# A decode step of four interleaved layers: the second attention layer's first queries split by key head, and a wider down product in the first feed-forward block

## The chip, the cores and the metric

The kernel runs on one core of one Trainium2 chip. The metric is the device time of one execution in microseconds; lower is better.

## The reference

Four layers run one after another on a residual `x` of 4 batch elements, one position each, 512 wide: attention, feed-forward, attention, feed-forward. Both attention layers use the same weights and the same key and value cache, and so do both feed-forward layers.

```python
def _A_ref(x, k_cache, v_cache, wq, wo):      # x [4, 1, 512]
    q = (x @ wq).reshape(B, Sq, 32, 128).transpose(0, 2, 1, 3)
    k = jnp.repeat(k_cache, 4, axis=1)        # caches [4, 8, 4096, 128]
    v = jnp.repeat(v_cache, 4, axis=1)
    scores = jnp.einsum("bhqd,bhkd->bhqk", q, k) * (128 ** -0.5)
    p = _softmax(scores, axis=-1)
    o = jnp.einsum("bhqk,bhkd->bhqd", p, v)
    return o.transpose(0, 2, 1, 3).reshape(B, Sq, 4096) @ wo

def _B_ref(x, w_gate, w_up, w_down):          # 512 -> 1792 -> 512
    return (_gelu(x @ w_gate) * (x @ w_up)) @ w_down

x = x + _A_ref(_layernorm(x), ...)
x = x + _B_ref(_layernorm(x), ...)
x = x + _A_ref(_layernorm(x), ...)
x = x + _B_ref(_layernorm(x), ...)
```

All inputs are bf16. Each batch element has 8 key heads of 4096 positions; four query heads share a key head.

## The kernel before, in words

**Order of the work.** An element depends on no other, so the kernel goes element by element: attention of element 0 (`attend_first`), its feed-forward block (`dense_first`), then `attend`, which does layer 3 of element 0 and layer 1 of element 1 together, then element 1's feed-forward block, and so on. Keys of an element stay in SBUF between its two attention layers; most values are read twice. The order of all instructions on each engine is the order in which they are written; the program doesn't reorder them.

**Tiles.** The 8 key heads of an element are two groups of four (`GH`). A head's 4096 positions are two tiles, `t = 0` and `t = last = 1`, of 128 x 2048 bf16 (512 KB). A key tile, once loaded, is transposed in place by VectorE (`Keys.turn`, L537). `place` says in which buffer (`kw`, `kp`) a tile lives; `own` in `Early` keeps the places of element 0, whose tiles are still to be used when element 1's tiles have been given a place. `Keys.load` issues a load on SP's queue (L518), the V ring does so at L708. Loads of one queue are issued in order. Eight semaphores go round, so at most eight loads are outstanding.

**Scores.** `scores_of` (L592) multiplies tiles by masked queries in `qb`: four matmuls (`be`) for each head and tile, of 512 columns each, and head `s` of a group writes partitions 32s to 32s+31 of the bank `sc`. For a run of several heads the loop goes over `be` outside and heads inside. The masked queries come in three steps: `q_round` (L335) subtracts the mean's part and rounds on VectorE, `q_sums_of` (L353) makes 16 small matmuls with the identity, and `q_spread` (L360) multiplies by a mask on VectorE. `soft` is the softmax: L602 reduces `sc`, and L614 takes the exponentials.

**Around the change.** `dense_first` ends with `down`: 14 blocks of four matmuls (L275) that add `wd_sb` times `H_bf` into a PSUM tile `y2`. `wide` repeats the right side to 32 equal columns, of which one is used. `wd_sb` is loaded in five pieces that end after blocks 6, 10, 12, 13 and 14 (`WD_PARTS`). Then element 0's second layer begins. `Early` serves this one place: before `queries`, three key tiles of element 1 have been loaded into buffers that had been parked elsewhere, and no further load can be issued until scores of element 0 have read a tile. `queries` makes the queries of the first group: heads 2 and 3 of the group with 32 matmuls, then heads 0 and 1 with 32. `scores` lets the scores of tile 0 of heads 2 and 3 go first, loads two tiles of element 1 into their places, finishes the masked queries of heads 0 and 1 (`rest`), makes the second group's queries (`qy`, L309), scores the other tiles and issues three more loads; it also brings parked tiles back with copies on VectorE, GpSimd and ScalarE (L565, L568, L570).

`Norm` holds the layer norm of one element: its constructor copies the mean, `root` (two VectorE and two ScalarE instructions) makes the inverse root, `scales` the two factors that the softmax uses.

`acc` takes a PSUM bank of two that go round; `y2`, the queries' sums, `sc` of the first group and the second group's query rows all come from it.

Of the kernel before, what the change touches and what calls it, by code (L numbers as in the profile page):

```python
# [15 lines left out]
P = 128  # L16
# [4 lines left out]
WIDE = 32  # L21
WEIGHT = 64
# [3 lines left out]
GH = 4  # L26
# [4 lines left out]
WD_PARTS = (0, 6, 10, 12, 13, 14)  # L31
# [5 lines left out]
def kernel(  # L37
# [15 lines left out]
    _, Hkv, Sk, Dh = A_k_cache.shape  # L53
    HqDh = A_wq.shape[1]
    Hq = HqDh // Dh
    rep = Hq // Hkv
    F = B_w_gate.shape[1]
    assert B == RUN and Sq == 1 and Dh == P and rep == QD and Hkv % GH == 0
    KD = D // P
# [31 lines left out]
    wq_sb = [wts.tile([P, KD, HG * Dh], BF16, name=f"wq_sb{g}") for g in range(NG)]  # L91
# [3 lines left out]
    wd_sb = wts.tile([P, KF, D], BF16, name="wd_sb")  # L95
# [28 lines left out]
    def k_tile(i, t):  # L124
        pair, n = place[i, t]
        return pair[:, n]

    def acc(shape, name, t=None):
        if t is None:
            t = ps_ac.tile([P, 512], FP32, name=name, tag="acc")  # L130
        n = 1
        for s in shape:
            n *= s
        if len(shape) == 1:
            return t[:, :n]
        return t[:, :n].rearrange("p (a b) -> p a b", b=shape[1])

    def wide(v, width=WIDE):
        n = v.shape[-1]
        return v.unsqueeze(1).broadcast_to([P, width // n, n])  # L140
# [133 lines left out]
    def mac(dst, lhsT, rhs, first, last):  # L274
        nc.tensor.matmul(dst, lhsT=lhsT, rhs=rhs, start=first, stop=last, skip_group_check=True)  # L275
# [54 lines left out]
    def q_tile():  # L330
        return grp.tile([P, HG], BF16, name="q_bf", tag="q_bf", bufs=1)

    def q_round(q_bf, q, g, norm, h0=0):
        own = slice(h0, h0 + q.shape[1])
        nc.vector.scalar_tensor_tensor(out=q_bf[:, own], in0=cs_q[:, g, own], scalar=norm.mean,  # L335
                                       in1=q[:, :, 0], op0=ALU.mult, op1=ALU.subtract)
# [4 lines left out]
    def q_sum_tile():  # L341
        return ps_sm.tile([P, GH, BE, rep], FP32, name="qe", tag="sm")

    def q_sums(q):
        qe = q_sum_tile()
        q_sums_of(qe, q, 0, GH)
        return qe

    def q_sums_of(qe, q, s0, n):
        iv = ident_bf[:].rearrange("p (b w e) -> p b e w", b=NB, e=2)  # L350
        for be in range(BE):
            for a in range(QD):
                nc.tensor.matmul(qe[a * QS:(a + 1) * QS, s0:s0 + n, be], lhsT=iv[:, be // 2, be % 2],  # L353
                                 rhs=q[:, s0 * rep:(s0 + n) * rep], start=True, stop=True,
                                 skip_group_check=True)

    def q_spread(qe, s0=0, n=GH):
        dst = qb[:, W:].rearrange("p (n x a h) -> p n x a h", x=2, a=QD, h=rep)[:, :, 0]
        shape = [P, n * BE, QD, rep]
        nc.vector.tensor_tensor(  # L360
            out=dst[:, s0 * BE:(s0 + n) * BE],
            in0=qe[:, s0:s0 + n].rearrange("p s n h -> p (s n) h").unsqueeze(2).broadcast_to(shape),
            in1=amask.unsqueeze(1).unsqueeze(3).broadcast_to(shape),
            op=ALU.mult)
# [11 lines left out]
    class OutProj:  # L376
# [8 lines left out]
        def heads(self, h0, n):  # L385
            for i in range(h0, h0 + n):
                for k in range(KD):
                    mac(self.full[:, k], wo_sb[:, i, k * P:(k + 1) * P],
                        wide(self.o(i), self.width),
                        self.n == 0 and k == 0, self.n == Hq - 1)  # L390
                self.n += 1
# [91 lines left out]
                             stop=start, skip_group_check=True)  # L483

    def down(nb, H_bf, whole):
        y = acc([KD, WIDE], "y2", whole)
        for c in range(KF):
            for k in range(KD):
                mac(y[:, k], wd_sb[:, c, k * P:(k + 1) * P], wide(H_bf[:, c, :]),
                    c == 0 and k == 0, c == KF - 1)  # L490
        return y[:, :, :nb]

# [89 lines left out]
    def scores(sc, g, t, runs=together):  # L582
        for run in runs:
            scores_of(sc, g, [(s, t) for s in run])

    def scores_of(sc, g, run):
        for be in range(BE):
            for s, t in run:
                n = s * BE + be
                w0 = n * 2 * W + (W if t == 0 else 0)  # L590
                kt = k_tile(g * GH + s, t).rearrange("p c (b j e) -> p c b j e", b=NB, e=2)
                nc.tensor.matmul(sc[s * QS:(s + 1) * QS], lhsT=qb[:, w0:w0 + 2 * W],  # L592
                                 rhs=kt[:, :, be // 2, :, be % 2],
                                 start=(t == 0 and be == 0),
                                 stop=(t == NT - 1 and be == BE - 1))
# [443 lines left out]
    class Early:  # L1039
# [15 lines left out]
            self.keys.load(1)  # L1055

        def queries(self, b, st):
            g, half = self.gx, GH // 2
            n = half * rep
            norm = Norm(st)  # L1060
            norm.root()
            q_bf, qs = q_tile(), []

            def heads(h0, h1):
                for i in range(h0, h1):
                    for k in range(KD):
                        mac(qs[-1][:, i % n], wq_sb[g][:, k, i * Dh:(i + 1) * Dh],
                            wide(xb[:, k, :RUN]), k == 0, k == KD - 1)

            qs.append(acc([n, WIDE], "q"))  # L1070
            heads(n, 2 * n)
            q_round(q_bf, qs[0][:, :, b:b + 1], g, norm, n)
            qs.append(acc([n, WIDE], "q"))
            heads(0, n // 2)
            qe = q_sum_tile()
            q_sums_of(qe, q_bf[:], half, half)
            heads(n // 2, n)
            q_spread(qe, half, half)
            q_round(q_bf, qs[1][:, :, b:b + 1], g, norm)

            def rest():
                q_sums_of(qe, q_bf[:], 0, half)
                q_spread(qe, 0, half)
                norm.scales()

            self.rest = rest
            return norm

        def scores(self, sc, qy, norm):
            gx, gy, own, keys = self.gx, self.gy, self.own, self.keys  # L1090
            a, c, last = gx * GH, gy * GH, NT - 1

            def home(i, t, freed):
                place[i, t] = own[freed]
                return k_tile(i, t).rearrange("p c d -> p (c d)")

            def load(i, t, freed):
                home(i, t, freed)
                assert keys.tile(keys.nl) == (i, t)
                keys.load(1)  # L1100

            def first(run):
                now = {(a + s, t): place[a + s, t] for s, t in run}
                place.update({k: own[k] for k in now})
                scores_of(sc, gx, run)
                place.update(now)

            first([(2, 0), (3, 0)])
            load(a + 3, 0, (a + 2, 0))
            load(a, last, (a + 3, 0))  # L1110
            self.rest()
            q = qy()
            first([(2, last), (3, last), (0, 0), (1, 0)])
            load(a + 1, last, (a + 2, last))
            load(a + 2, last, (a + 3, last))
            to = home(c + 1, last, (a + 1, 0))
            self.one.back(to, 1, nc.vector)
            self.one.back(to, 2, nc.gpsimd)
            self.two[0].back(home(c + 2, last, (a, 0)), 2)
            first([(0, last), (1, last)])  # L1120
            load(a + 3, last, (a, last))
            to = home(c + 3, last, (a + 1, last))
            self.two[1].back(to, 1)
            other = new_scores()

            def build():
                qe = q_sums(q)
                busy(4, other.rearrange("p c j -> p (c j)"))
                q_spread(qe)

            p0 = soft(sc, norm, meanwhile=build)
            self.two[1].back(to, 1, nc.vector)
            return p0, other
# [347 lines left out]
    y, early, scr = attend_first()  # L1481
    prev = NoValues()
    for b in range(B):
        y = dense(b, y, prev, Scratch()) if b else dense_first(y, scr)
# [6 lines left out]
        if b == 0:  # L1491
            ring.pump()
            norm = early.queries(b, st)
        else:
            q_bf = q_tile()
            if b == B - 1:
# [7 lines left out]
                rest, steps = acc([HG, WIDE], "q"), q_steps(b, gy)  # L1504
# [3 lines left out]
            norm = Norm(st)  # L1508
# [4 lines left out]
            qe = q_sums(q_bf[:])  # L1513
# [10 lines left out]
            else:  # L1524
                q_bf = q_tile()
# [6 lines left out]
        def qy(b=b, g=gy, norm=norm):  # L1532
            q_bf = q_tile()
            q_round(q_bf, turn_rows(q_rows(b, g)), g, norm)
            return q_bf[:]

        if b < B - 1:
            y, prev = attend(b + 1, qy, prev, norm, early if b == 0 else None)
        else:
            y, full, squares = attend_last(q_bf, norm, prev, late[3 * NT:])  # L1540
# [32 lines left out]
```

## Time and profile before

| | us |
|---|---|
| runs of the kernel | 268.29, 269.05, 269.88 (median 269.05) |
| the profiled execution's own time | 268.99 |
| its span, first to last instruction | 267.2 |
| TensorE, VectorE, ScalarE busy | 195.1 (73%), 182.2 (68%), 66.0 (25%) |
| read from HBM | 102.50 MB, 384 GB/s over the span |
| mean granted TensorE clock | 0.866 |

The profile is one execution. Times in it count from the span's start. A row of the page's slices has 40 digits, one for 6.68 us, in tenths busy; PEclk is the granted clock in tenths. In a windows answer each line is a stretch with busy time and instruction count of PE, PEld, DVE, ACT and POOL, then granted clock, share of the DMA engines and GB/s. A line of waits has the total, the number and the longest, in us. A piece of the chain has start and duration. A timeline line has start, duration, engine, line, operation and tile.

### The profile page before, as it was taken

To read this page: it belongs to the slowest core of one execution; us is meant where nothing else is said; L and a number is where in the kernel's file an instruction comes from. 1 tells how busy PE (TensorE), PEld (TensorE's weight loads), DVE (VectorE), ACT (ScalarE), POOL (GpSimd) and SP (SyncE) were. 2 spreads that over 40 slices of the span, in tenths; PEclk is the share of its full clock that TensorE was granted. 3 is DMA by queue.
4 is the path that set the end of the run, shared out by engine and by line. 5 is a ranking of instruction groups with operands and counts; after the bars stand their busy time and mean duration, and the time that the engine had idled before them with its cause. 6 is when DMAs were issued, how large, how long until landed. Compare 5 with 4: busy or idle time off the path is not lost.

```text
span 267.2 us, 8596 instructions
## 1 busy us (share of the span) xinstructions
PE 195.1 (73%) x3767; PEld 114.8 (43%) x3775; DVE 182.2 (68%) x448; ACT 66.0 (25%) x136; POOL 3.9 (1%) x10
## 2 busy tenths in 40 slices
PE   1396246544689796989678968787788687888884
PEld 1333123322255453557436245464363354553563
DVE  3385955451335899884776998746769996568773
ACT  1001001100222422032323520304136103044642
POOL 2000000000001000000000000000000000000001
PEclk9998555655597959799999985899999979999999
DMA  7999999999994999999999999999999999999940
GB/s 244 432 416 421 423 429 417 408 385 406 413 412 177 394 416 417 420 417 400 390 414 416 416 419 421 416 415 375 403 418 418 421 415 418 420 405 405 413 160 3
DMA packets 30732, 103.05 MB, mean 386 GB/s; under 512 B 2788, under 2 KB 7144, under 8 KB 29672
## 3 DMA queue, kind: packets, MB, share of 16 engines
q1 hardware_dynamic: 30672, 102.51, 95.7%
q8 instruction: 29, 0.48, 0.6%
q14 instruction: 7, 0.06, 0.1%
q10 hardware_dynamic: 24, 0.01, 0.0%
HBM read 102.50 MB, written 0.00 MB: 384 GB/s over the span
## 4 chain that ended last, share of the span: by engine, by line
DMA 51%; PE 21%; DVE 16%; SPq 6%; ACT 3%; issue 3%; DVEq 0%
DMA v_t<-in_A_v_cache_dram 25%; DMA kp<-in_A_k_cache_dram 8%; DMA kw<-in_A_k_cache_dram 8%; PE sc L592 6%; DMA wu_sb<-in_B_w_up_dram 5%; DMA kw<-in_A_v_cache_dram 4%; SPq L161 4%; DVE kp L537 3%; PE ot L859 3%; DVE kw L537 3%; PE y L275 3%; PE so L791 2%; PE q L309 1%; DVE q L315 1%; DVE qb L360 1%
## 5 line engine op out<-in xcount | busy, mean ns | idle before, releaser
L592 PE MATMUL sc<-kw,qb 128*32 128x512 bf16 x244 | 39.6, 446 | 5.2 <-DVE kw L537 2.2
L592 PE MATMUL sc<-kp,qb 128*32 128x512 bf16 x268 | 40.1, 450 | 1.0 <-DVE kp L537 0.2
L592 PEld LDWEIGHTS <-qb 128*32 128x32 bf16 x512 | 23.1, 104 | 39.6 <-issue 21.4
L537 DVE STREAM_TRANSPOSE kw<-kw 128x1024 f32<-128x1024 f32 x32 | 38.0, 1215 | 0.7 <-DMA kw<-in_A_k_cache_dram 0.6
L537 DVE STREAM_TRANSPOSE kp<-kp 128x1024 f32<-128x1024 f32 x32 | 36.7, 1199 | 0.0
L859 PE MATMUL ot<-pe,v_t 128*128 128x32 bf16 (+1 forms) x896 | 30.0, 184 | 5.6 <-DMA v_t<-in_A_v_cache_dram 2.8
L859 PEld LDWEIGHTS <-v_t 128*128 128x128 bf16 x896 | 27.7, 100 | 13.7 <-issue 7.4
L614 ACT ACTIVATE pe<-sc,nl 128x512 bf16<-128x512 f32 x8 | 5.5, 687 | 85.9 <-DVE pe L611 67.6
L791 PE MATMUL so<-v_t,pe 128*32 128x256 bf16 x304 | 15.0, 319 | 13.6 <-DMA v_t<-in_A_v_cache_dram 11.6
L799 DVE STREAM_TRANSPOSE so<-so 128x512 f32<-128x512 f32 (+1 forms) x23 | 13.8, 599 | 11.1 <-PE so L791 11.1
L791 PEld LDWEIGHTS <-pe 128*32 128x32 bf16 x320 | 9.1, 105 | 19.4 <-issue 12.5
L602 DVE TENSOR_REDUCE pe<-sc 128x1 f32<-128x512 f32 x12 | 8.3, 691 | 9.2 <-PE sc L592 9.1
L405 PE MATMUL yr<-wo_sb,OT_bf 128*2 128x512 bf16 (+1 forms) x120 | 10.7, 425 | 4.9 <-DMA wo_sb<-in_A_wo_dram 4.9
L647 PE MATMUL x<-pe,ident_bf 128*32 128x128 bf16 x192 | 5.4, 233 | 11.8 <-DVE pe L622 11.8
L647 PEld LDWEIGHTS <-ident_bf 128*32 128x32 bf16 x256 | 5.3, 100 | 16.1 <-issue 14.1
L791 PE MATMUL so<-v_t,pl 128*32 128x256 bf16 x192 | 9.4, 275 | 3.3 <-DMA v_t<-in_A_v_cache_dram 3.3
L650 ACT CAST pe<-x 128x512 bf16<-128x512 f32 x12 | 7.0, 586 | 17.4 <-PE x L647 17.4
L275 PE MATMUL q<-xb,wq_sb 128*128 128x5 bf16 (+1 forms) x192 | 5.7, 173 | 6.5 <-DMA wq_sb<-in_A_wq_dram 6.5
L353 PE MATMUL qe<-q_bf,ident_bf 128*32 128x16 bf16 (+1 forms) x272 | 5.7, 176 | 5.6 <-DVE q_bf L335 2.9
L622 DVE STREAM_TRANSPOSE pe<-pe 128x512 bf16<-128x512 bf16 x12 | 8.4, 696 | 1.1 <-ACT pe L614 1.1
L275 PEld LDWEIGHTS <-wo_sb 128*128 128x128 bf16 x160 | 7.6, 101 | 3.3 <-DMA wo_sb<-in_A_wo_dram 2.6
L482 PEld LDWEIGHTS <-ident_bf 128*128 128x128 bf16 x63 | 5.2, 99 | 8.7 <-issue 4.3
(172 smaller groups left out, 255.2 us busy)
## 6 DMA issues: line engine op xcount, KB each, us to landing
v_t<-in_A_v_cache_dram SPq DMA_DIRECT2D x89, 512.0 KB, 8.5
kp<-in_A_k_cache_dram SPq DMA_DIRECT2D x32, 512.0 KB, 9.9
kw<-in_A_k_cache_dram SPq DMA_DIRECT2D x24, 512.0 KB, 9.6
wq_sb<-in_A_wq_dram SPq DMA_DIRECT2D x2, 2048.0 KB, 7.7
kw<-in_A_k_cache_dram SPq DMA_DIRECT2D x4, 1024.0 KB, 11.6
v_t<-in_A_v_cache_dram SPq DMA_DIRECT2D x4, 1024.0 KB, 14.2
wo_sb<-in_A_wo_dram SPq DMA_DIRECT2D x4, 1024.0 KB, 12.0
wq_sb<-in_A_v_cache_dram SPq DMA_DIRECT2D x3, 1024.0 KB, 11.8
```

The lines of the kernel that those rows point to most:

```text
L161: dq.dma_start(out=wo_sb[:, i * n:(i + 1) * n], in_=wo_dram[:, i * n:(i + 1) * n])
L275: nc.tensor.matmul(dst, lhsT=lhsT, rhs=rhs, start=first, stop=last, skip_group_check=True)
L405: nc.tensor.matmul(self.rows[j:j + x.shape[1]], lhsT=x, rhs=wo_sb[:, i], start=self.n < QD, stop=True, skip_group_check=True)
L537: nc.vector.transpose(out=words, in_=words)
L592: nc.tensor.matmul(sc[s * QS:(s + 1) * QS], lhsT=qb[:, w0:w0 + 2 * W], rhs=kt[:, :, be // 2, :, be % 2], start=(t == 0 and be == 0), stop= ...
L602: nc.vector.tensor_reduce(out=m, in_=sc.rearrange("p c j -> p (c j)"), axis=AX.X, op=ALU.min if norm else ALU.max)
L622: nc.vector.transpose(out=flat, in_=flat)
L647: nc.tensor.matmul(x[a * QS:(a + 1) * QS, s], lhsT=ident_bf[:, s * QS:(s + 1) * QS], rhs=pT[:, a], start=True, stop=True, skip_group_check ...
L650: nc.scalar.copy(out=pe, in_=x.rearrange("p s t c h -> p (s t c h)"))
L791: nc.tensor.matmul(ps[d, :NW * QS], lhsT=x[:, w:w + NW].rearrange("p c h -> p (c h)"), rhs=v[:, i:i + NW, d], start=first and i == 0, stop ...
L799: nc.vector.transpose(out=flat, in_=flat)
L859: nc.tensor.matmul(self.ot[:, s % 2], lhsT=v[:, i, :], rhs=wide(pe[:, s, t * CH + i, :], self.ot.shape[-1]), start=(done == 0 and i == 0), ...
```

## The change

In `down` the first ten blocks stream 64 equal columns (`WEIGHT`) instead of 32. In `Early.queries` the first query matmuls are those of head 3 alone (16), then those of head 2 (16); each head has its own rounding, sums and spread. Heads 0 and 1 (32 matmuls), `root` and head 2's sums and spread move into a step `second`, which runs after the first scores. In `Early.scores` tile 0 of head 3 is scored alone and its own buffer is reloaded at once; then come `second`, the scores of head 3's other tile and of head 2's first tile, two loads, the sums and spread of heads 0 and 1 (`others`), and the rest as before. Element 1's tiles are loaded in the same order as before, the second and third into other buffers.

```diff
     def down(nb, H_bf, whole):
-        y = acc([KD, WIDE], "y2", whole)
+        y = acc([KD, WEIGHT], "y2", whole)
         for c in range(KF):
+            n = WEIGHT if c < WD_PARTS[2] else WIDE
             for k in range(KD):
-                mac(y[:, k], wd_sb[:, c, k * P:(k + 1) * P], wide(H_bf[:, c, :]),
+                mac(y[:, k, :n], wd_sb[:, c, k * P:(k + 1) * P], wide(H_bf[:, c, :], n),
                     c == 0 and k == 0, c == KF - 1)
...
         def queries(self, b, st):
-            g, half = self.gx, GH // 2
-            n = half * rep
+            g, half, last = self.gx, GH // 2, GH - 1
             norm = Norm(st)
-            norm.root()
-            q_bf, qs = q_tile(), []
-
-            def heads(h0, h1):
-                for i in range(h0, h1):
+            q_bf = q_tile()
+
+            def heads(q, s0):
+                for i in range(q.shape[1]):
+                    h = s0 * rep + i
                     for k in range(KD):
-                        mac(qs[-1][:, i % n], wq_sb[g][:, k, i * Dh:(i + 1) * Dh],
+                        mac(q[:, i], wq_sb[g][:, k, h * Dh:(h + 1) * Dh],
                             wide(xb[:, k, :RUN]), k == 0, k == KD - 1)
 
-            qs.append(acc([n, WIDE], "q"))
-            heads(n, 2 * n)
-            q_round(q_bf, qs[0][:, :, b:b + 1], g, norm, n)
-            qs.append(acc([n, WIDE], "q"))
-            heads(0, n // 2)
+            def rounded(q, s0):
+                q_round(q_bf, q[:, :, b:b + 1], g, norm, s0 * rep)
+
+            def spread(s0, n):
+                q_sums_of(qe, q_bf[:], s0, n)
+                q_spread(qe, s0, n)
+
+            qs = []
+            for s in (last, last - 1):
+                qs.append(acc([rep, WIDE], "q"))
+                heads(qs[-1], s)
+            rounded(qs[0], last)
             qe = q_sum_tile()
-            q_sums_of(qe, q_bf[:], half, half)
-            heads(n // 2, n)
-            q_spread(qe, half, half)
-            q_round(q_bf, qs[1][:, :, b:b + 1], g, norm)
-
-            def rest():
-                q_sums_of(qe, q_bf[:], 0, half)
-                q_spread(qe, 0, half)
+            q_sums_of(qe, q_bf[:], last, 1)
+            rounded(qs[1], last - 1)
+            q_spread(qe, last, 1)
+            rest = acc([half * rep, WIDE], "q")
+
+            def second():
+                spread(last - 1, 1)
+                heads(rest, 0)
+                rounded(rest, 0)
+                norm.root()
+
+            def others():
+                spread(0, half)
                 norm.scales()
 
-            self.rest = rest
+            self.second, self.others = second, others
             return norm
...
-            first([(2, 0), (3, 0)])
-            load(a + 3, 0, (a + 2, 0))
-            load(a, last, (a + 3, 0))
-            self.rest()
+            first([(3, 0)])
+            load(a + 3, 0, (a + 3, 0))
+            self.second()
+            first([(3, last), (2, 0)])
+            load(a, last, (a + 3, last))
+            load(a + 1, last, (a + 2, 0))
+            self.others()
             q = qy()
-            first([(2, last), (3, last), (0, 0), (1, 0)])
-            load(a + 1, last, (a + 2, last))
-            load(a + 2, last, (a + 3, last))
+            first([(2, last), (0, 0), (1, 0)])
+            load(a + 2, last, (a + 2, last))
```

## The prediction

> **What bounds the kernel now.** I read the page's slices first. The DMA row is full almost everywhere, and the one dip in the middle is slice 13, which begins at 80.2 us:
>
> ```profile
> PEclk9998555655597959799999985899999979999999
> DMA  7999999999994999999999999999999999999940
> ```
>
> The kernel reads 102.5 MB and is bound by that stream; a hole in it is paid unless something later was waiting anyway. Microsecond windows show the hole, and TensorE at half clock in it (the last columns are granted clock, DMA share, GB/s):
>
> ```profile
> 80.00:81.00 1.00, 1.00 (x48) 0.95 (x45) 0.44 (x2) 0.38 (x2) 0.00 (x0) 0.50 0.59 234
> 81.00:82.00 1.00, 1.00 (x18) 0.44 (x16) 0.30 (x2) 0.00 (x0) 0.00 (x0) 0.50 0.16 66
> 82.00:83.00 1.00, 1.00 (x20) 0.42 (x20) 0.00 (x0) 0.00 (x0) 0.00 (x0) 0.50 0.00 0
> 83.00:84.00 1.00, 1.00 (x30) 0.73 (x28) 0.41 (x3) 0.00 (x0) 0.00 (x0) 0.93 0.00 0
> 84.00:85.00 1.00, 1.00 (x22) 0.54 (x14) 0.83 (x2) 0.00 (x0) 0.00 (x0) 1.00 0.84 291
> 85.00:86.00 1.00, 1.00 (x25) 0.60 (x22) 0.89 (x3) 0.90 (x1) 0.84 (x2) 1.00 0.87 340
> ```
>
> The waits of SP's queue name the cause: the L518 key loads wait for TensorE's first scores, which release the tiles to be reloaded.
>
> ```profile
> SPq L518 <- PE qe L353: 7.6, 2, 7.5
> SPq L518 <- PE sc L592: 3.3, 3, 1.8
> ```
>
> In the single records the five loads issue at 83.10, 83.52, 85.02, 85.44 and 85.92, the next at 88.10; the first packet moves at 84.07, 0.97 after its issue. From then to the last value tile (landed 258.28) the stream does not run dry: from the load of 85.44 on I counted three or more outstanding loads at every issue up to the last. A tile of 512 KB at 417 GB/s takes 1.25 us.
>
> **The clock.** The next fence is a windows answer cut at the clock's steps; they lie on a grid of 3.41 us:
>
> ```profile
> 76.30:79.72 3.42, 2.95 (x86) 2.40 (x86) 0.92 (x5) 0.00 (x0) 0.00 (x0) 1.00 1.06 421
> 79.72:83.13 3.41, 3.41 (x90) 2.21 (x90) 0.90 (x4) 0.41 (x2) 0.00 (x0) 0.50 0.30 121
> ```
>
> TensorE was busy for 2.95 us and yet lost its clock. I counted columns instead: matmul by matmul, those running side by side on different quarters of the columns counted once, from 0.1 us after the recorded start, as a share of what a window can stream at full clock (512 columns start 0.216 us apart). In all 63 windows from 18.3 us on, those followed by half clock hold at most 0.356, those followed by full clock at least 0.371. The window above holds 0.356.
>
> **Part 1, down's wider sums.** 40 of the 56 matmuls of `down` stream 64 columns instead of 32. That adds 1280 columns or 0.156 of a window: 0.51, well over the border, so I expect full clock from 79.72. Their own time is hidden by the last weights; in the chain of waits the sums run in three pieces:
>
> ```profile
> 76.64 1.15 PE y L275 x40
> 77.81 0.60 PE y L275 x12
> 78.46 0.28 PE y L275 x4
> ```
>
> Blocks 10, 12 and 13 start at 77.82, 78.15 and 78.46, each 0.05 after its piece of `wd_sb` landed (77.77, 78.11, 78.41). Now 40 start 25 ns apart. With 64 columns from four equal copies, as `H_bf` has them, 16 take 0.65 including a 0.19 tail, so 31 ns each:
>
> ```profile
> 124.31 0.65 PE L275 MATMUL y<-OL_bf,wo_sb 128*128 128x64 bf16 x16
> 130.83 0.40 PE L791 MATMUL so<-v_t,pl 128*32 128x256 bf16 x8 [0.59 <-DMA v_t<-in_A_v_cache_dram]
> ```
>
> (The second line is for later.) 40 x 31 = 1.23 us ends at 77.87, eight more at 78.07, before block 12 lands: cost 0. Without that cover it is 0.23; at the 57 ns of 64 columns from a single copy (the 128x64 row at 178.06) it would be about 0.6. I take 0.
>
> **Part 2, one head first,** at full clock, from the start of the queries at 79.10. Before, 32 q matmuls stood ahead of the first rounding, now 16: last start 79.48, end 79.66. Rounding (L335, 0.22 after 0.04) 79.91; sums (16 of L353, 0.28 after 0.10) 80.29; head 2's rounding stands ahead of the spread on VectorE, 80.09 to 80.31; spread (L360: 0.41 for 256 columns, 0.29 for 128, so an estimated 0.23 for 64) 80.60; scores from 80.70. A head's scores go to its own quarter: the two heads of before went in four steps 0.427 apart (81.18, 81.59, 82.01, 82.44), which is one 512-column pass each at half clock. One head also needs four steps: it saves no scoring time, only the clock does. Last start 81.35, 0.39 to its end, 0.03 to SP: first load 81.77 instead of 83.10, **1.33 earlier**.
>
> Then come head 2's sums (0.1), the 32 q matmuls of heads 0 and 1 (0.8, to 82.45) and four paired steps (0.86): second load 83.53, third 83.95 (0.42 apart as now), instead of 83.52 and 85.02. Sums, qy's rows (0.86) and four steps of three heads (0.86): fourth load 85.4 as before. Four paired steps more: the softmax reduction starts at 86.3, not 85.92. In all TensorE has four passes more (16, not 12: 0.86) and 16 sums more (0.1), VectorE a rounding and a spread (0.45). While the first scores wait for their spread, TensorE stands for some 0.5 us with all its later work behind them; those times contain it.
>
> `root` moves behind the rounding of heads 0 and 1: two VectorE operations (0.21, 0.16) and two on ScalarE (0.20 each), done by about 83.9; its last reader, L611, ran at 87.34: cost 0, 0.8 without that cover. SP keeps the order of its loads, and nothing else is queued between them; POOL's copy L568 starts 0.3 later and has its reader at 87.9: 0.
>
> **The sum.** The first tile flows from 82.74 to 84.0; the others follow at 84.50, 0.5 late. Later loads arrive in time (fourth 86.4, needed at 87.0). That equals an unbroken stream from 84.50 - 1.25 = 83.25 instead of 84.07: **-0.8**. Filling the queue costs something: from 84 to 88 the share was 0.84, 0.87, 0.95, 1.05 against 1.03, a loss of 0.41. Doing it twice costs 0 to 0.4; I take **+0.2**. The softmax is 0.38 later and VectorE is nearly solid from 89 to 113, so this travels on to q's rows at 131, where TensorE waited 0.59 for a value tile (last fence): covered, 0, or 0.38 if not. Sum -0.6 against the profiled execution's 268.99 (span 267.2, 1.8 around it; the median of the runs is 269.05): **268.4**, between 267.8 and 268.9.
>
> The Trainium skill's page "TensorE: Matmul & The Clock Gate" ("Why this matters for your kernels") asks for no TensorE-idle gaps over about 3 us, and its Part 1 has the clock drop after an idle window. By that rule the 76.3 window, busy 2.95 of 3.42 us, was no case for a drop, and more columns per matmul would cure nothing. The trace disagrees: the clock dropped. By that rule the sum would be rival A's.
>
> **Rivals.** A, slower: the half clock stays and the softmax path decides. For it: the margin is thin just after 80.4. Had the grid put a window's end at 80.7, the changed kernel would hold about 0.39 there, with 0.371 the lowest that held. At 0.427 a step the first load issues at 82.66, the second at 84.5, and the softmax starts at 87.25, 1.33 late. That exceeds the 0.59 at 131 by 0.74, value slots come free later, and the short queue (three to four outstanding from 125 to 136) runs thin: at 132 to 134 it gave 369 GB/s where 417 is usual, 11%, or up to 1.35 over those 12 us. +0.75 to +2.1, middle **270.4**. It decides once the softmax is over 0.6 late. Against: 0.51 is far over the border on this grid.
>
> B, nothing: the lead is spent again. A window ending between 78.9 and 79.8 holds under 0.36 in the kernel before; one ending elsewhere keeps the clock. Then the old order itself, at 0.216 a step, loads at 82.23, its stream runs from 83.2 unbroken, and the change wins 0.05. The four extra passes are all that is left: **269.0**. For it: the times agree to 0.6%, as if phases mixed. The same page's Part 1 calls the window free-running, not tied to a kernel's start; one profile can't show it.
>
> C, more than forecast: the early tile also spares the slow filling. Then the 1.33 counts whole and the 0.41 vanishes, -1.7: **267.3**. For it: the first tile's packets start alone and the other loads find the queue awake. Against: the 0.5 us between first and second load.
>
> **How the numbers follow.** Forecast 0.33, C 0.30, A 0.25, B 0.12. The 0.5% that a measurement of this kernel can tell from no change is 1.35 us: below 267.7 lies C with 0.03 of the forecast's tail, 0.33; above 270.4 lies 0.19 of A, 0.19; the rest 0.48. The range takes in C's lower end with some scatter and the middle of A: 266.8 to 270.6.
>
> **What would show it.** Right: clock 1.00 from 79.7 to 83.1, first load near 81.8, second near 83.5, a DMA share near 1 in 83 to 84 and a short dip behind it, the reduction L602 near 86.3, q's rows at 131 no later than now. Wrong: half clock in the first scores (A), a first load after 82.3, an empty DMA second between the first and second tile, or the wait at 130.8 replaced by one for VectorE.

## The result: 0.7% slower

The changed kernel takes 270.51 us (median of 21 runs, 269.08 to 271.67), the kernel before 268.58 beside it (21 runs); the ratio is 1.0073 with a 95% interval of 1.0057 to 1.0088. The forecast was 268.4, a gain, so the sign was wrong. The profiled execution has a span of 268.41 us and a time of its own of 270.51.

Nearly every event that the prediction placed came where it was placed. The page's slices, as before (40 slices of 6.71 us, tenths):

```profile
PEclk9999559555599958999999997899999957999999
DMA  6999999999996999999999999999999999999940
```

The dip in the DMA row is at the same slice, and less deep (6 for 4). Microsecond windows, columns as before (busy time and count of PE, PEld, DVE, ACT, POOL, granted clock, DMA share, GB/s):

```profile
81.00:82.00 1.00, 1.00 (x24) 0.60 (x22) 0.00 (x0) 0.00 (x0) 0.00 (x0) 1.00 0.23 94
82.00:83.00 1.00, 1.00 (x36) 0.86 (x36) 0.36 (x3) 0.00 (x0) 0.00 (x0) 1.00 0.18 33
83.00:84.00 1.00, 1.00 (x32) 0.68 (x31) 0.37 (x3) 0.41 (x2) 0.00 (x0) 1.00 0.89 311
84.00:85.00 1.00, 1.00 (x24) 0.70 (x17) 0.59 (x4) 0.00 (x0) 0.00 (x0) 1.00 0.89 250
85.00:86.00 1.00, 1.00 (x19) 0.58 (x15) 0.96 (x3) 0.26 (x1) 0.20 (x1) 1.00 0.76 262
```

The clock is full where it was half, and the second from 83 to 84, empty before, moves 311 GB/s. But the next two move 250 and 262, where the kernel before had 291 and 340 after a later start. The clock's windows in this run lie elsewhere (cut at its own grid):

```profile
74.80:78.20 3.40, 2.59 (x51) 1.53 (x44) 1.46 (x5) 0.10 (x1) 0.00 (x0) 1.00 1.06 410
78.20:81.60 3.40, 2.97 (x96) 2.20 (x93) 1.15 (x6) 0.00 (x0) 0.00 (x0) 1.00 0.78 318
```

In SP's waits for the same loads (L519 now) the wait for the first scores is down from 7.5 us at the longest to 6.0.

```profile
SPq L519 <- PE qe L353: 8.4, 3, 6.0
```

`down` is one piece in the chain of waits, no longer three with the last weights between them, and the residual `xb` behind it starts at 78.96 (78.76 before):

```profile
77.14 1.80 PE y L275 x56
```

What the forecast's sum did not have (rival A did) is further on. The stretch that holds element 1's first values, in the windows of before, then after:

```profile
120.00:146.00 26.00, 21.46 (x537) 13.94 (x526) 16.67 (x58) 7.12 (x15) 0.00 (x0) 1.00 1.02 404
```

```profile
120.00:146.00 26.00, 21.34 (x539) 14.37 (x532) 17.05 (x57) 7.12 (x15) 0.00 (x0) 1.00 1.01 388
```

16 GB/s of 404 over 26 us is 1.0 us of stream. The value products in the changed kernel's timeline (start, duration, what; idle before them and its releaser at the end) show TensorE's side of it: where one wait of 0.59 us stood at 130.8, two stand at 133.6 and 134.9, together 1.96. q's rows themselves, between these, start at 131.18, 0.13 later than before. The value loads of the stretch issue later: those that SP issued at 125.34 and 132.66 before go out at 125.97 and 134.08.

```profile
130.47 0.86 PE L792 MATMUL so<-v_t,pl 128*32 128x256 bf16 x16
133.64 0.40 PE L792 MATMUL so<-v_t,pl 128*32 128x256 bf16 x8 [1.23 <-DMA v_t<-in_A_v_cache_dram]
134.86 0.40 PE L792 MATMUL so<-v_t,pl 128*32 128x256 bf16 x8 [0.73 <-DMA v_t<-in_A_v_cache_dram]
```

Summing the bytes that had landed, I took the times at which each kernel reached the amounts that the kernel before had at 80, 120, 146, 176, 200 and 232 us. The table gives the time that each then spent on the same bytes (one profile each; the last column runs to the last byte; labels are those of the experiments below):

| kernel | to 80 | 80-120 | 120-146 | 146-176 | 176-200 | 200-232 | 232-end |
|---|---|---|---|---|---|---|---|
| before | 80.00 | 40.00 | 26.00 | 30.00 | 24.00 | 32.00 | 33.91 |
| changed | 80.12 | 39.87 | 26.99 | 30.01 | 24.25 | 32.01 | 33.85 |
| e1, down's columns alone | 80.06 | 39.76 | 26.02 | 30.02 | 23.42 | 32.01 | 34.49 |
| e3, four zero steps | 80.00 | 39.57 | 25.88 | 30.05 | 23.87 | 32.01 | 33.72 |
| e3, eight zero steps | 79.92 | 40.63 | 27.21 | 29.99 | 23.98 | 32.01 | 34.09 |
| e7, no early tile | 79.96 | 41.29 | 26.05 | 30.01 | 24.57 | 32.01 | 35.12 |
| e9, split, shorter queries | 80.02 | 39.93 | 25.88 | 30.03 | 23.65 | 32.09 | 35.38 |

The changed kernel is 0.12 us behind at 80 us, has made that good by 120, loses 0.99 from 120 to 146 and 0.25 from 176 to 200, and ends 1.2 later. The values of one profile in the last column scatter by more than a microsecond, and I draw nothing from a single one of them. The stretch from 120 to 146 scatters too: e4 below, which turned out to do the same work at the same times as the changed kernel, takes 26.43 us there and not 26.99.

### The profile page after: what moved, and what is told of

The parts are those of the page before. It is cut to its first block, busy times and chain, and to the rows that moved or that the text cites. A ratio compares the mean times of both kernels' runs of the same rounds, so it can differ in the third digit from the quotient of the medians.

```text
span 268.4 us, 8630 instructions
## 1 busy us (share of the span) xinstructions
PE 193.1 (72%) x3783; PEld 114.6 (43%) x3791; DVE 182.4 (68%) x450; ACT 66.0 (25%) x136; POOL 3.9 (1%) x10
## 4 chain that ended last, share of the span: by engine, by line
DMA 56%; PE 23%; DVE 11%; SPq 5%; ACT 2%; issue 2%; DVEq 0%
DMA v_t<-in_A_v_cache_dram 29%; DMA kw<-in_A_k_cache_dram 10%; DMA kp<-in_A_k_cache_dram 8%; PE sc L593 6%; DMA wg_sb<-in_B_w_gate_dram 5%; DMA kw<-in_A_v_cache_dram 4%; SPq L161 4%; PE ot L860 3%; PE y L275 3%; DVE kp L538 3%; PE so L792 2%; DVE kw L538 2%; PE q L309 1%; PE y L482 1%; DVE q L315 1%
## 5 line engine op out<-in xcount | busy, mean ns | idle before, releaser
L593 PE MATMUL sc<-kw,qb 128*32 128x512 bf16 x244 | 38.7, 436 | 5.2 <-DVE kw L538 2.5
L353 PE MATMUL qe<-q_bf,ident_bf 128*32 128x16 bf16 (+2 forms) x288 | 6.4, 175 | 4.9 <-DVE q_bf L335 2.2
L360 DVE TENSOR_TENSOR qb<-qe,masks 128x256 bf16<-128x256 f32 (+2 forms) x17 | 6.4, 376 | 3.9 <-PE qe L353 3.7
```

## The experiments

Two theories. **Theory 1:** the early bytes are worth little; the first softmax of element 0's second layer comes too late, everything that VectorE and TensorE do behind it comes late with it, and value slots come free too late to keep the queue full from 120 us on. **Theory 2:** the split order itself costs, with its reloads scattered in time. All ratios are to the kernel before run beside each (three chips, on which it took 268.2 to 268.7 us).

**The two parts apart (e1, e2).** e1 is the kernel before with the new `down`; e2 is the changed kernel with the old one:

```diff
-        y = acc([KD, WEIGHT], "y2", whole)
+        y = acc([KD, WIDE], "y2", whole)
         for c in range(KF):
-            n = WEIGHT if c < WD_PARTS[2] else WIDE
             for k in range(KD):
-                mac(y[:, k, :n], wd_sb[:, c, k * P:(k + 1) * P], wide(H_bf[:, c, :], n),
+                mac(y[:, k], wd_sb[:, c, k * P:(k + 1) * P], wide(H_bf[:, c, :]),
```

> The kernel before with the wider down alone; the queries and loads keep their old order. Theory 1, the late softmax decides: with full clock the first load issues near 82.2 and the softmax reduction starts near 85.1 instead of 85.92, so value slots come free earlier and nothing is lost in 120 to 140; 0.5 to 1.0 us faster than the kernel before (267.6 to 268.1). Theory 2, the scattered reloads decide: the loads stay in pairs, so it also wins, by the 0.9 that the stream starts earlier. Rival 3, the wider sums themselves cost: slower than before by 0.3 or more.

> The changed kernel with down at 32 columns: the split alone. If the clock halves in the first scores: first load near 82.7, softmax near 87.2. Theory 1: the softmax is later than in the changed kernel, so it is slower than that by 0.5 or more (1.2% over before). Theory 2: the loads are as scattered as in the changed kernel: same time as that within 0.3 us. If the clock stays up, the same as the changed kernel by both.

e1: 268.60 us, 1.0012 (0.9985 to 1.0039). e2: 270.40, 1.0081 (1.0054 to 1.0107). So the loss is the split's, and the wider sums are worth nothing that shows, where both theories had forecast a gain of 0.5 us or more: e1's profile has full clock from 75.0 to 92.0 and its first load at 82.50 instead of 83.10. e2 had full clock in its profile too, with the old 32 columns. How often the kernel before has half clock in this place is not known from its one profile.

**The old order with a late softmax (e3).** e1 with zero matmuls ahead of the last paired scores, eight, four and six steps of two; the first four loads stay:

```diff
+            for _ in range(8):
+                for s in range(2):
+                    mac(sc[s * QS:(s + 1) * QS], qb[:, 0:1].broadcast_to([P, QS]), some,
+                        False, False)
             first([(0, last), (1, last)])
```

> The wider down alone, and 8 matmuls of zeros (512 columns each) put into each of two quarters of the first group's score bank between the loads and the last four paired score steps: 1.7 us of TensorE work that changes no number and moves none of the first four loads. The softmax reduction goes from about 85.1 to about 86.9. Theory 1: 1.0 to 2.0 us slower than the kernel with the wider down alone, about as slow as the changed kernel. Theory 2: within 0.3 us of the kernel with the wider down alone.

> The old order with down's 64 columns, and four steps of zero matmuls (two matmuls of 512 columns each, adding zeros to the scores) between the third load's release and the last paired score steps: half as many as in the run with eight steps. The first four loads stay at 82.4 to 84.7 us; the softmax reduction starts near 86.1 us instead of 85.25. Theory 1 (the late softmax decides) expects about half of what eight steps cost: 0.5 to 1.5 us over the kernel with down's columns alone (268.6), so 269.1 to 270.1. Theory 2 (the scattered reloads decide) expects 268.6, within 0.3.

> The old order with down's 64 columns and six steps of zero matmuls in front of the last paired scores, between the four that cost nothing (ratio 1.001, reduction at 85.95 us) and the eight that cost 1.1% (86.90). The reduction starts near 86.4, where the changed kernel has it; the first four loads stay. Theory 1: the change's whole loss without its split, ratio 1.005 to 1.010. Theory 2: no more than 1.003.

Four steps (reduction at 85.95 us): 268.48 us, 1.0010 (0.9983 to 1.0037). Six (86.12): 269.73, 1.0049 (1.0029 to 1.0069). Eight (86.90): 271.15, 1.0108 (1.0083 to 1.0134). A late softmax alone, without a split query, costs as much as the whole change and more; the first 0.7 us over e1's 85.25 cost nothing that shows. The forecast for four steps by theory 1 (half the loss) was wrong: it is a cover that ends, not a slope from zero. The stretch from 120 to 146 us says the same, four steps, six and eight:

```profile
120.00:146.00 26.00, 22.05 (x532) 14.59 (x528) 17.27 (x57) 7.49 (x16) 0.00 (x0) 0.97 1.02 406
```

```profile
120.00:146.00 26.00, 21.21 (x539) 14.38 (x528) 17.07 (x58) 7.20 (x16) 0.00 (x0) 1.00 1.01 389
```

```profile
120.00:146.00 26.00, 20.44 (x486) 12.93 (x476) 15.83 (x55) 6.54 (x13) 0.00 (x0) 1.00 0.99 385
```

**Why the softmax is late.** VectorE's timeline, the changed kernel and then e1:

```profile
84.82 0.73 DVE L315 STREAM_TRANSPOSE q<-q 128x512 f32<-128x512 f32 x1 [0.37 <-PE q L309]
85.59 0.23 DVE L335 SCALAR_TENSOR_TENSOR q_bf<-cs_q,ln,q 128x16 bf16<-128x16 f32 x1
85.77 0.69 DVE L566 TENSOR_SCALAR kp<-park 128x512 int32<-128x512 int32 x1
86.54 0.69 DVE L603 TENSOR_REDUCE pe<-sc 128x1 f32<-128x512 f32 x1
```

```profile
83.48 0.73 DVE L315 STREAM_TRANSPOSE q<-q 128x512 f32<-128x512 f32 x1 [0.37 <-PE q L309]
84.25 0.23 DVE L335 SCALAR_TENSOR_TENSOR q_bf<-cs_q,ln,q 128x16 bf16<-128x16 f32 x1
84.50 0.69 DVE L566 TENSOR_SCALAR kp<-park 128x512 int32<-128x512 int32 x1
85.25 0.69 DVE L603 TENSOR_REDUCE pe<-sc 128x1 f32<-128x512 f32 x1
```

In both, VectorE is busy almost without a gap from the second group's query rows (L315) to the reduction. What is late is L315, by 1.34 us: TensorE makes those rows behind the split's extra passes. The second reduction follows 5.7 us behind the first in both (92.27, 90.99), so the lateness is handed on.

**The early tile (e4, e7).** By the diff of the change, each of the first four reloads takes another buffer than in the kernel before. e4 moves the first reload's instruction behind the paired scores; e7 exchanges the buffers of the first two reloads, so that the first one has to wait for those scores:

```diff
-            load(a + 3, 0, (a + 3, 0))
             self.second()
             first([(3, last), (2, 0)])
-            load(a, last, (a + 3, last))
+            load(a + 3, 0, (a + 3, last))
+            load(a, last, (a + 3, 0))
```

> The changed kernel, but the first load is issued with the second and third, behind the paired steps (about 83.8 instead of 81.9); all engines' work stays in its order. Theory 1: the softmax isn't moved and the early tile's lead was lost anyway by 96 us: within 0.3 us of the changed kernel. Theory 2 in its strict form, that a lone tile disturbs the filling of the queue: faster than the changed kernel by 0.3 or more. If the early tile was worth its 1.0 us to the end: slower by 0.7 to 1.2.

> The changed kernel with the buffers of its first and second reload exchanged: the first reload now really waits for the paired score steps and issues near 83.8 us instead of 81.87, together with the second. The work on TensorE and the softmax stay where the changed kernel has them (reduction near 86.5). It measures what the early tile is worth. Theory 1 expects almost nothing: within 0.4 us of the changed kernel (270.1 to 270.9), since the lead was gone by 96 us there. If an early byte is an early end, as the prediction had it, it is slower than the changed kernel by 0.7 to 1.2 us (271.2 or more).

e4 missed its purpose: SP's queue has nothing ahead of the load, which waits only for the scores of its own buffer, and it issued at 81.50 as ever. It is a second measurement of the changed kernel: 270.53 us, 1.0101 (1.0071 to 1.0130). e7's loads issue at 84.35 and 84.73: 270.27 us, 1.0056 (1.0025 to 1.0086). A first tile 2.5 us later (2.0 counted from `xb`, which is 0.5 later in this profile) costs nothing that shows. The stretch from 84 to 92 us in the changed kernel and in e7, and e7's from 120 to 146:

```profile
84.00:92.00 8.00, 7.27 (x136) 3.94 (x127) 6.82 (x16) 4.51 (x7) 1.16 (x2) 1.00 0.96 340
```

```profile
84.00:92.00 8.00, 7.33 (x130) 3.77 (x127) 6.30 (x16) 4.91 (x9) 1.17 (x2) 1.00 0.84 305
120.00:146.00 26.00, 22.03 (x546) 14.10 (x535) 17.31 (x58) 7.12 (x15) 0.00 (x0) 1.00 1.02 404
```

e7's stream is 1.3 us late at 120 (41.29 in the table) and then loses nothing up to 146; the changed kernel's is on time and loses 0.99 there. At 146 the two stand 0.3 apart, with the softmax 7.58 and 7.60 us behind `xb`. I read it so: the stream can run ahead only until the value slots are full, and from then on goes at the pace at which they are released.

**Taking the lateness back (e6, e8, e9).** e6 makes element 0's second-group queries from one contraction step of four; e9 does so for heads 0 and 1 as well; e8 moves 16 query matmuls into TensorE's wait before the first scores:

```diff
-            q_round(q_bf, turn_rows(q_rows(b, g)), g, norm)
+            rows_of_q = streamed("q", HG, q_steps(b, g)[:1]) if b == 0 else q_rows(b, g)
+            q_round(q_bf, turn_rows(rows_of_q), g, norm)
...
-                heads(rest, 0)
+                heads(rest, 0, 1)
```

> The changed kernel, but the second group's query rows of element 0 are made from one of their four contraction steps (three quarters of that sum are left out), so that TensorE has 24 matmuls fewer between the first scores and the last ones. The order of loads stays as changed; the first three loads stay where they were (81.8, 83.8, 84.2 us), the fourth and fifth and the softmax come about 0.65 us earlier (reduction near 85.9). Theory 1 expects most of the loss to vanish: within 0.3% of the kernel before (at most 269.2). Theory 2 expects it to stay: ratio 1.007 or more (270.2 or more).

> The changed kernel with 16 of the 32 query matmuls of heads 0 and 1 moved ahead of the first scores, into the wait of TensorE for the first spread (80.25 to 80.8 us). The first load stays near 81.87 or comes up to 0.1 later; everything behind the first scores comes 0.4 us earlier: second and third load near 83.4 and 83.85, softmax reduction near 86.1. Theory 1 expects it 0.4 to 1.0 us faster than the changed kernel (269.5 to 270.1). Theory 2, for which the scattered loads themselves cost, expects no more than 0.3 us.

> The changed kernel with shorter queries of element 0: the second group's query rows and the first group's heads 0 and 1 are each made from one of their four contraction steps (three quarters of these sums are left out), so that TensorE has 24 + 24 = 48 matmuls fewer between the first scores and the last ones. The order of the split, of its loads and of VectorE's work stays. First load 81.8 us, second and third near 83.3, softmax reduction near 85.7, inside the 0.7 us that the run with four zero steps showed to be free. Theory 1 (the softmax chain's lateness decides, what exceeds about 0.6 us is paid): back at the kernel before, ratio at most 1.003. Theory 2 (the split order of the reloads itself costs): 1.007 again.

e6: 270.79 us, 1.0084 (1.0054 to 1.0115). e8: 270.23, 1.0076 (1.0053 to 1.0100). Both missed their softmax: the reduction came at 86.34 and 86.27, not 85.9 and 86.1, so they tell little. e9 hit it (85.85), and the loss from 120 to 146 is gone:

```profile
120.00:146.00 26.00, 21.01 (x525) 13.73 (x522) 16.46 (x56) 7.12 (x15) 0.00 (x0) 0.99 1.02 406
```

Yet it took 270.05 us, 1.0059 (1.0037 to 1.0082). Theory 1 alone does not give that.

**Earlier loads in the old order (e10, e11).** On e1: tile 1 of heads 2 and 3 is scored right behind their tile 0, and in e11 the second group's query rows are also made behind the softmax:

```diff
+            first([(2, last), (3, last)])
+            load(a + 1, last, (a + 2, last))
+            load(a + 2, last, (a + 3, last))
             self.rest()
             q = qy()
-            first([(2, last), (3, last), (0, 0), (1, 0)])
+            first([(0, 0), (1, 0)])
```

> The old order of the queries with down's 64 columns, but tile 1 of heads 2 and 3 is scored at once behind their tile 0, ahead of the masked queries of heads 0 and 1 and of the second group's queries. It moves the third and fourth load forward by about 1.0 us (to 83.4 and 83.8 from 84.4 and 84.8); the first two (82.5, 82.9), the fifth (85.3) and the softmax reduction (85.25) stay. Theory 1: the stream gets earlier and the softmax not, so the same as the kernel with down's columns alone (268.6) within 0.3%. If an early stream is worth what the prediction gave it, 0.5 to 1.0 us faster (267.6 to 268.1).

> The kernel with the pairs first, and in addition the second group's query rows are made behind the softmax of the first group instead of ahead of its last scores: the fifth load comes near 84.3 us, the softmax reduction near 84.4 (0.85 earlier), the second group's masked queries 0.8 later. Theory 1: a gain only if the second group's scores, not the first softmax, have slack on the chain; between 267.5 and 268.6. If the second group's queries are what sets the chain, slower: 269.0 to 270.0.

e10: 269.89 us, 1.0051 (1.0025 to 1.0076). The third and fourth load issue at 83.79 and 84.22, 0.6 earlier than in e1, but the softmax, meant to stay, is 0.9 later behind the four extra steps (7.09 us after `xb`, e1 6.19). e11: 271.26 us, 1.0104 (1.0068 to 1.0141): its first reduction is in time (85.92, though 84.4 was meant), its second at 92.49, 1.5 later than e1's. It is the chain behind the softmax, not the first reduction as such, that has to be in time.

**The same work left out in both orders (e12 to e17).** e12 is e9 with two of four steps of the middle scores left out; e13 the old order with all that left out; e14 is e12 with e7's exchange; e15 is e13 with six zero steps. e16 and e17 are e9 and e15 once more.

```diff
-            first([(2, last), (0, 0), (1, 0)])
+            first([(2, last), (0, 0), (1, 0)], 2)
```

> The changed kernel with three quarters of two query sums of element 0 left out (as in the run with shorter queries), and of the middle scores of the first group (head 2's tile 1, heads 0 and 1's tile 0) two of four steps left out. First load 81.8 us, second and third 83.2 and 83.6, fourth 84.3, softmax reduction near 85.5. Theory 1 (lateness decides): the same as the old order with the same work left out and its softmax delayed to the same time, within 0.3%, and at most 1.003 of the kernel before. Theory 2 (the split order costs by itself): 0.4% or more over that run, 1.006 of the kernel before.

> The old order with down's 64 columns and the same work left out as in the light split kernel. First two loads 82.3 and 82.7 us as before, third and fourth about 0.9 earlier (83.5, 83.9), softmax reduction near 84.3, 0.9 earlier than with all work. Theory 1 with a cover of 0.6 us: an earlier softmax gains nothing, 268.3 to 268.6 (ratio 0.999 to 1.001). If the chain is bound already in the kernel before: 0.3 to 0.9 us faster (0.9965 to 0.999).

> The light split kernel with the buffers of the first and second reload exchanged, so that the first reload waits for the paired scores (83.2 instead of 81.8 us); everything else as there. Theory 1: within 0.2% of the light split kernel. If the lone early tile costs (its queue is filled twice): faster than it by 0.2 to 0.5%. If an early tile is worth something: slower by 0.3 to 0.5%.

> The old order with the same work left out, and six steps of zero matmuls ahead of its last paired scores: softmax reduction near 85.6 us, where the light split kernel has it; loads as in the old light kernel up to the fourth. Theory 1: the same as the light split kernel within 0.3%, both at most 1.003 of the kernel before. Theory 2: this one at most 1.002 and the split one 1.006.

> The split kernel with shorter queries once more, the same file as before (three quarters of two query sums of element 0 left out). Theory 1 (only lateness decides, the loss behind 232 us belonged to that run's clock windows): the stretch from 120 to 146 us again takes about 26.0 us, the one from 232 us to the last byte 33.0 to 33.8 unless half clock falls at 220 to 231 again; ratio at most 1.004. Theory 2 (the split order itself costs): 1.006 again, with 34 us or more behind 232 us whatever the clock.

> The old order with the work of the light split kernel left out and six steps of zero matmuls, once more (the same file as before): ratio 1.002 to 1.005, on the same chip as the split kernel with shorter queries. Theory 1: within 0.3% of that one. Theory 2: at least 0.3% below it.

| kernel | first load | reduction, us after `xb` | GB/s 120-146 | ratio (95%) |
|---|---|---|---|---|
| e13 old, light | 82.47 | 5.50 | 400 | 1.0033 (1.0007 to 1.0059) |
| e1 old | 82.50 | 6.19 | 404 | 1.0012 (0.9985 to 1.0039) |
| e14 split, light, no early tile | 83.15 | 6.48 | 395 | 1.0051 (1.0023 to 1.0080) |
| e12 split, light | 81.69 | 6.50 | 400 | 1.0048 (1.0017 to 1.0080) |
| e17, e15 old, light, late | 82.24 | 6.81, 6.82 | 399, 403 | 1.0025 (0.9997 to 1.0054), 1.0034 (1.0004 to 1.0065) |
| e16, e9 split, short | 81.70, 81.83 | 6.93 | 399, 406 | 1.0059 (1.0035 to 1.0084), 1.0059 (1.0037 to 1.0082) |
| e3 old, four steps | 82.35 | 7.03 | 406 | 1.0010 (0.9983 to 1.0037) |
| e8 split | 82.00 | 7.26 | 393 | 1.0076 (1.0053 to 1.0100) |
| e6 split | 81.82 | 7.44 | 395 | 1.0084 (1.0054 to 1.0115) |
| e3 old, six steps | 82.09 | 7.45 | 389 | 1.0049 (1.0029 to 1.0069) |
| changed | 81.87 | 7.58 | 388 | 1.0073 (1.0057 to 1.0088) |
| e2 split | 81.84 | 7.61 | 389 | 1.0081 (1.0054 to 1.0107) |
| e4 split | 81.50 | 7.64 | 398 | 1.0101 (1.0071 to 1.0130) |
| e3 old, eight steps | 82.41 | 7.92 | 385 | 1.0108 (1.0083 to 1.0134) |

Rows are in the order of the lateness, counted from the start of `xb` in the same profile. Two things stand in the table. With a late softmax the stretch from 120 to 146 us is slower, in both orders: 399 to 406 GB/s in the upper rows but for e14, 385 to 395 from e8 on but for e4. (Not in the table: e7, late as a stream already; e10, 363 GB/s with half clock from 133.8 to 140.7 us; e11, 393 with its second reduction late; and the kernel before, 7.16 us and 404 with its first scores at half clock.) Where the fall lies is known only as between 7.16 us (the kernel before) and 7.44 (e6): e8 has half clock inside the stretch, from 135.8 to 139.2 us. And the groups overlap by the scatter of one kernel: the changed kernel and e4 have 388 and 398, e9 and e16 (one file) 406 and 399.

And the time does not follow that alone: split kernels with their softmax in time are still 0.5 to 0.6% slower, old ones with work left out 0.25 to 0.34%, old ones with all their work 0.1%. At about the same lateness split and old differ by 0.34% (e16 against e17, run side by side, 1.0059 and 1.0025) and by 0.14% (e12 and e15, 1.0048 and 1.0034), and these intervals overlap. Both theories missed forecasts: theory 1 those for e9, e13 and e16, theory 2 those for e3's eight and six steps, e12 and e15; e16 came out as theory 2 had it. So a late softmax is enough for a loss of this size, and it is the only cause tried here with which the stretch from 120 to 146 slowed down in the old order; but taking the lateness back did not bring the split's time back, and a cost of the split order itself of 0.1 to 0.3% is not excluded.

e9 and e16 take 35.38 and 34.81 us behind 232 us against 33.91 before, but so do e15 and e17 (34.77 and 35.15), with half clock until 230.9 us in e9 and e17, but only until 223.9 and 217.9 in e16 and e15: where the rest is lost I could not settle. That less work (e13) comes out 0.2% behind e1 is within their intervals and stays unexplained as well. No version beat the kernel before.

## Why the prediction was wrong

**Full clock came, but not by the wider sums, and it was worth nothing that shows.** The clock was full from 74.8 to 95.2. By a recount of streamed columns, as in the prediction, the windows from 74.8 and from 78.2 hold 0.65 and 0.53; those of e2, with the old columns, 0.54 and 0.50, and it kept the clock too. So on these grids nothing needed curing. The border came out again in the changed kernel (at most 0.36 ahead of half clock, at least 0.37 ahead of full); but the kernel before has 73 windows, not 63, and by the recount one near its end, from 257.2, held 0.33 and was followed by full clock. In one profile of the kernel before the window's end fell badly, and I took that profile for the kernel. e1's sums gained nothing. The Trainium skill's page "TensorE: Matmul & The Clock Gate" (Part 1) calls the window free-running; the profiles agree: the half clock ahead of this place ends at 72.9, 74.8, 73.2 and 75.0 us in four of them (before, changed, e3 with eight steps, e1). Rival B had said so and I gave it 0.12.

**The schedule held.** First load 81.77 predicted, 81.87 measured; second 83.53 and 83.84; fourth 85.4 and 85.70; reduction 86.3 and 86.54. 0.20 of each difference is `xb`, which started that much later. The wide sums' cost of 0 was not right: it rested on a cover by the last weights. In e1 and e2 `down` starts at the same 77.23, so late that the weights no longer hold it up, and takes 1.80 with the wide sums and 1.66 without: 0.14, inside the 0.23 that the prediction gave for no cover.

**The filling term was mis-sized.** The lead was put at 0.8 and a second filling at 0.2, net 0.6; from 80 to 120 us the stream gained 0.13. With one to three loads outstanding, 84 to 86 us moved 250 and 262 GB/s, and 84 to 92 moved 340 against 370 before.

**There was no cover: this is the step that turned the sign.** The sum took the softmax's "0.38 later" as "covered, 0", by the 0.59 that TensorE waited at 130.83 for a value tile. But the load of that very tile stands behind the softmax. The kernel before's chain of waits, from the first scores to the issue of that load at 125.34, runs through engines alone, without a transfer in it:

```profile
124.96 0.33 PE so L791 x8
125.34 5.46 DMA v_t<-in_A_v_cache_dram
130.83 0.40 PE so L791 x8
```

In the changed kernel the first reduction is 0.62 later (0.42 counted from `xb`), the second 0.64, the fourth, at 114.58, 0.77, and this load 0.63 (125.97). The next load, 126.62 before and 127.25 now, is also 0.63 later, and lands 1.61 later (133.60 instead of 131.99): the lateness was handed on whole, and a slower stream added to it.

A cover there is, but ahead of this load, and in the profile that the prediction read the first scores at half clock had used it up. At full clock the old order reduces at 85.25 (e1), 0.67 earlier. Its load still goes out at 125.34, for on the way its chain waits for another value tile, loaded from 113.67 on, and from there (120.75) TensorE is no earlier than before (120.76):

```profile
113.67 7.05 DMA v_t<-in_A_v_cache_dram
```

From that base four zero steps show 0.7 as free, and the changed kernel is 1.29 later, so about 0.6 should have been charged. That the cover read off the wrong wait, 0.59, is near 0.7 is luck.

**Rival A had the mechanism and the wrong trigger.** It charged a softmax over 0.6 late with a thin queue at 125 to 136 us and +0.75 to +2.1; measured is 0.99 from 120 to 146 and 1.2 over the span. (Its own sign, a softmax over 0.6 late, was just met: 0.62.) But A let this happen only if the half clock stayed, so 0.25 went to a case that did not occur while its price was paid in the case that did. No rival had a full clock and a late softmax together.

**Rival C fell.** A first tile 2.5 us later costs nothing that shows (e7 against the changed kernel, 1.0056 and 1.0073; e14 against e12, 1.0051 and 1.0048), so the early one spares nothing.

## What to carry to other kernels

Where a stream is held in step by buffers that a later computation frees, ask of an earlier transfer how far it can run ahead before those buffers fill, and of a later computation by how much it passes its cover: here a first load 2 us earlier bought nothing, and about 0.6 us beyond the cover went with up to a microsecond of stream lost 40 us later. A wait for a transfer is a cover only if the transfer's issue doesn't hang on the same chain: follow the load back to what released it. Ask of the base of a comparison whether its profile shows a chance event: one whose clock window fell badly hid 0.7 us of lateness. When extra passes are put ahead of a long chain, follow the first VectorE instruction that waits for them, not only the load that they release.

## What the runs showed of the hardware

The rate of the stream went with the number of 512 KB loads outstanding: in 2 us stretches from 84 to 256 us of six profiles (before, changed, e1, e2, e3 with eight steps, e4), with loads counted from issue to last landing, two to three outstanding gave about 250 GB/s, three to five 380 to 390, five and more 407 to 414. The first figure is from four stretches alone, all from 84 to 86 us and so right behind an empty queue, and three to four gave anything from 330 to 410: that the number of loads sets the rate is not shown.

A load's 16 parts can land far apart: one value tile of the changed kernel landed between 133.48 and 137.61 us, the same one before between 133.54 and 134.70.
